# Eight chunks of a scan-and-adapters kernel: loads in 4 KB rows with woven 64-row transposes, and a re-searched order of its instructions

## The chip, the core and the metric

The kernel runs on 1 core of a Trainium2 chip. The metric is the device time in microseconds, the median of several runs. A profiled execution gives the times of single instructions.

## What is computed

The reference takes `a` and `b` of shape 8 x 6400 x 128 and runs a recurrence along the second axis. Its output `x`, seen as 51200 rows of 128, then goes through a mixture of eight adapters of rank 16, of which each row uses its two best:

```python
for t in range(S):
    h = a[:, t] * h + b[:, t]
    out[:, t] = h
...
logits = x @ w_gate
topk = np.argpartition(-logits, 2, axis=1)[:, :2]
w = softmax of the two selected logits
out = x + sum over the two of w[k] * ((x @ A[e]) @ B[e])
```

Input is 52.4 MB (`a` and `b`), output 26.2 MB.

## The kernel before

The 51200 rows are 100 chunks of 512. A chunk c goes through these steps, each an operation with a short name in the program (line numbers are those of the profile, which are the lines of the kernel before):

| name | engine | line | what |
|---|---|---|---|
| la, lb | SyncE queue | L710 | loads of a and b; from chunk 4 on, one load of 512 KB brings two chunks |
| A, B, P | TensorE | L731 | transposes of a into bank pA, of b into bank pB |
| ae | ScalarE | L749 | copy of pA into a_st |
| sc | VectorE | L787 | the scan over 512 steps: xT from a_st and pB; it needs the scan of the chunk before |
| Z | TensorE | L807 | xT times [A, w_gate] for a unit of 6 blocks of 128 rows, into pZ |
| ze | ScalarE | L813 | copy of pZ into zl |
| gate steps | VectorE, GpSimd, ScalarE | L844 to L883 | for a group of up to 4 units: the largest and the second largest logit, the weights g (sigmoid on ScalarE) |
| mu or md | GpSimd (L916) or VectorE (L920) | | product zw of zl and g |
| T | TensorE | L929 | transpose of zw into bank pO |
| te | VectorE (L938) or ScalarE (L935) | | copy of it into zwT |
| D | TensorE | L943, L944 | xT transposed back plus zwT times B, into pO |
| oe or od | ScalarE (L958) or VectorE (L955) | | copy of pO into outt |
| st | SyncE queue | L989 | store; one store of 512 KB takes two chunks, the last four chunks go one by one |

Of the gate steps, the two maxima and the last step (g, L883) are VectorE's; the others (kinds 2, 3, 5, 6 and 7: L844 to L875) are GpSimd's, but for those named in `GATE_DVE`. `TE_ACT`, `MU_DVE` and `OE_DVE` name the chunks whose zwT copy is ScalarE's, whose product is VectorE's, and whose outt copy is VectorE's.

Two layouts of a load occur (`load`, L695; `pieces`, L716). A flat chunk has 4 rows of 512 bytes to a partition, 2 KB in one piece, and its transposes are 4 of 128 x 128. In a woven pair, 8 rows, 4 KB in one piece, go to a partition; the first chunk of the pair lies on partitions 0 to 63, the second on 64 to 127. A woven chunk's transposes are 8 with 64 rows, and those of b of a chunk are woven with those of a of the next one, which lies on the other half of the partitions, to run side by side. Which layout a chunk has is decided by one line (L692):

```python
def woven(c):
    return HEAD <= c < NCH - TAIL and c // HC not in FLAT
```

`HEAD` is 4, `HC` is 2, `TAIL` is 0 and `FLAT` is [2, 3, 4, 5], so chunks 0 to 3 are flat in single loads of 256 KB, chunks 4 to 11 flat in pairs, and the others woven. There are buffers for 6 pairs (`NL`): a load waits until the transposes have read the pair that was there before. In `front` (L751), P is the woven group; A and B are the flat ones.

The order of the instructions on each engine is that of a rank (`schedule`, L333), sorted engine by engine:

```python
rank[op.i] = op.base + (TEMPLATE[op.kind][op.k] if op.kind in TEMPLATE else 0.0) + NUDGE.get(op.name, 0.0)
```

`TEMPLATE` holds an offset for each kind of operation and place in a period of 6 chunks, `NUDGE` one for each single operation; both come from a search. Each engine runs its list in that order, and an operation that must wait holds up what stands behind it. SyncE issues loads and stores from one list too. The store of chunks 68 and 69 is split (`SPLIT`) into parts of 124 and 4 rows of partitions.

Of the kernel before, what the change touches and what calls it, by code (L numbers as in the profile page):

```python
# [219 lines left out]
EARLY = -400  # L220
LEAD = [1, 2]
TAPER = [2, 1, 1, 1, 1]
GATE_DVE = ['2_14', '2_17', '2_18', '2_21', '3_14', '3_16', '5_17', '6_21', '7_16', '7_17', '7_18', '7_20', '7_21']
TAIL_UNITS = [4, 4, 4, 4]
HEAD_UNITS = [4, 4, 4]
FLAT = [2, 3, 4, 5]
# [56 lines left out]
    "q6": [0.0],  # L283
    "q7": [0.0],
    "q8": [0.0],
    "g7": [0.0],
    "g8": [0.0],
}

# [818 lines left out]
```

## Time and profile before

| | us |
|---|---|
| median of 3 runs | 203.43 (203.04 to 203.93) |
| profiled execution | 202.69 |
| its span | 200.7 |
| VectorE busy | 176.5 |
| ScalarE busy | 172.7 |
| GpSimd busy | 140.5 |

A profile has several views. The page gives busy totals, the span in 40 slices, the DMA queues, the chain of waits that ended last and the costliest groups of instructions. The windows view gives busy time, DMA share and rate for chosen stretches. The timeline lists instructions by start. The DMA view, cut to a stretch, lists what was issued in it, with the time from issue to landing.

### The profile page before, as it was taken

To read this page: it belongs to the slowest core of one execution; us is meant where nothing else is said; L and a number is where in the kernel's file an instruction comes from. 1 tells how busy PE (TensorE), PEld (TensorE's weight loads), DVE (VectorE), ACT (ScalarE), POOL (GpSimd) and SP (SyncE) were. 2 spreads that over 40 slices of the span, in tenths; PEclk is the share of its full clock that TensorE was granted. 3 is DMA by queue.
4 is the path that set the end of the run, shared out by engine and by line. 5 is a ranking of instruction groups with operands and counts; after the bars stand their busy time and mean duration, and the time that the engine had idled before them with its cause. 6 is when DMAs were issued, how large, how long until landed. Compare 5 with 4: busy or idle time off the path is not lost.

```text
span 200.7 us, 7490 instructions
## 1 busy us (share of the span) xinstructions
PE 180.8 (90%) x3128; PEld 157.9 (79%) x3128; DVE 176.5 (88%) x287; ACT 172.7 (86%) x317; POOL 140.5 (70%) x182
## 2 busy tenths in 40 slices
PE   6978999999999999899989999988879999998980
PEld 6868877888788888788878888877767887887860
DVE  1579999999999999999999999987888989999980
ACT  2548898999999998999899998986988998998971
POOL 1314559997888899797989798979678677744200
PEclk9999999999999999999999999999999999999997
DMA  5999999999999999999999999999999999999995
GB/s 213 382 391 389 412 406 411 398 416 407 406 410 414 405 411 412 416 411 407 408 414 408 409 418 407 407 411 414 410 413 411 410 414 410 404 384 379 352 371 225
DMA packets 30089, 79.26 MB, mean 395 GB/s; under 512 B 2664, under 2 KB 2920, under 8 KB 30056
## 3 DMA queue, kind: packets, MB, share of 16 engines
q1 hardware_dynamic: 29480, 78.39, 99.2%
q8 instruction: 25, 0.41, 0.8%
q10 hardware_dynamic: 576, 0.40, 0.6%
q14 instruction: 8, 0.07, 0.1%
HBM read 52.56 MB, written 26.21 MB: 393 GB/s over the span
## 4 chain that ended last, share of the span: by engine, by line
PE 21%; DVE 18%; DMA 13%; POOL 7%; ACT 3%; issue 2%; SPq 0%; DVEq 0%
DVE xT L787 9%; DMA b_tm<-in_b_dram 7%; DMA a_tm<-in_a_dram 6%; PE pZ L807 4%; POOL zw L916 4%; PE pA L731 4%; PE pB L731 3%; PE pO L929 3%; DVE zw L920 3%; PE pO L943 3%; PE pO L944 3%; DVE zwT L938 2%; ACT zl L813 1%; POOL L L846 1%; DVE g L883 1%
## 5 line engine op out<-in xcount | busy, mean ns | idle before, releaser
L787 DVE TENSOR_TENSOR_SCAN xT<-a_st,xT,pB 128x512 f16<-128x512 f32 x96 | 120.3, 1253 | 7.8 <-PE pB L731 3.7
L916 POOL TENSOR_TENSOR zw<-zl,g 128x512 f16<-128x512 f32 x87 | 92.0, 1068 | 21.9 <-DVE g L883 18.8
L731 PE MATMUL pB<-ident_f,b_tm 64*128 64x64 f32 (+1 forms) x752 | 68.3, 232 | 2.1 <-DMA a_tm<-in_a_dram 1.0
L731 PE MATMUL pA<-ident_f,a_tm 64*128 64x64 f32 (+1 forms) x752 | 68.2, 232 | 1.7 <-DMA b_tm<-in_b_dram 1.3
L749 ACT COPY a_st<-pA 128x512 f32<-128x512 f32 x100 | 59.9, 608 | 8.3 <-PE pA L731 5.9
L731 PEld LDWEIGHTS pA<-ident_f,a_tm 64*128 64x128 f32 (+1 forms) x752 | 55.7, 140 | 6.8 <-DMA b_tm<-in_b_dram 2.4
L813 ACT COPY zl<-pZ 128x816 f32<-128x816 f32 (+1 forms) x69 | 57.8, 838 | 3.7 <-PE pZ L807 3.5
L731 PEld LDWEIGHTS pB<-ident_f,b_tm 64*128 64x128 f32 (+1 forms) x752 | 55.2, 139 | 7.0 <-DMA a_tm<-in_a_dram 1.7
L958 ACT COPY outt<-pO 128x512 f32<-128x512 f32 x91 | 54.3, 609 | 3.3 <-PE pO L944 2.6
L943 PE MATMUL pO<-ident_h,xT 128*128 128x128 f16 x368 | 51.0, 221 | 0.5 <-ACT zwT L935 0.2
L944 PE MATMUL pO<-cst_h,zwT 128*128 128x128 f16 x368 | 50.3, 219 | 0.0
L943 PEld LDWEIGHTS pO<-ident_h,xT 128*128 128x128 f16 x368 | 40.7, 113 | 2.5 <-ACT zwT L935 0.4
L807 PE MATMUL pZ<-cst_h,xT 128*128 128x136 f16 x400 | 36.0, 225 | 6.4 <-ACT zl L813 2.7
L929 PE MATMUL pO<-ident_h,zw 128*128 128x128 f16 x368 | 35.5, 220 | 2.1 <-ACT outt L958 1.3
L944 PEld LDWEIGHTS pO<-cst_h,zwT 128*128 128x128 f16 x368 | 36.5, 99 | 0.0
L807 PEld LDWEIGHTS pZ<-cst_h,xT 128*128 128x128 f16 x400 | 26.3, 115 | 11.6 <-DVE xT L787 4.3
L938 DVE COPY zwT<-pO 128x512 f16<-128x512 f16 x72 | 29.2, 408 | 2.4 <-PE pO L929 2.0
L929 PEld LDWEIGHTS pO<-ident_h,zw 128*128 128x128 f16 x368 | 22.6, 97 | 6.2 <-issue 1.5
L846 POOL TENSOR_SCALAR L<-k 128x192 f32<-128x192 f32 (+2 forms) x15 | 12.2, 810 | 3.2 <-DVE k L844 2.0
L935 ACT COPY zwT<-pO 128x512 f16<-128x512 f16 x20 | 11.9, 603 | 1.3 <-PE pO L929 1.0
L787 DVE TENSOR_TENSOR_SCAN xT<-a_st,pB 128x512 f16<-128x512 f32 (+1 forms) x8 | 7.5, 937 | 4.9 <-ACT a_st L749 4.7
L853 POOL TENSOR_TENSOR L<-k,m 128x192 f32<-128x192 f32 (+2 forms) x17 | 8.5, 500 | 2.5 <-DVE m L851 2.4
(56 smaller groups left out, 110.8 us busy)
## 6 DMA issues: line engine op xcount, KB each, us to landing
a_tm<-in_a_dram SPq DMA_DIRECT2D x48, 512.0 KB, 13.2
b_tm<-in_b_dram SPq DMA_DIRECT2D x48, 512.0 KB, 13.3
out_dram<-outt SPq DMA_DIRECT2D x47, 512.0 KB, 13.4
a_tm<-in_a_dram SPq DMA_DIRECT2D x4, 256.0 KB, 4.2
out_dram<-outt SPq DMA_DIRECT2D x4, 256.0 KB, 3.6
b_tm<-in_b_dram SPq DMA_DIRECT2D x3, 256.0 KB, 4.8
out_dram<-outt SPq DMA_DIRECT2D x1, 496.0 KB
b_tm<-in_b_dram ACTq DMA_DIRECT2D x1, 256.0 KB, 3.5
```

The costliest lines, as they stand in the source:

```text
L731: last = eng["pe"].transpose(*args)
L749: lambda: eng["act"].copy(a_st[c % NA][:, :], pA[:, c % 2, :]), fr(c, "ae"))
L787: last = eng["dve"].tensor_tensor_scan(out=x[:, s0:s1], data0=a_st[c % NA][:, s0:s1], data1=pB[:, c % 2, s0:s1], initial=init, op0=ALU.mul ...
L807: last = eng["pe"].matmul(pZ[:, k // (n // 2), o : o + W], xblock(b0 + k), Awg_h)
L813: return eng["act"].copy(zl[:, zb : zb + n, :].rearrange("p (h k) w -> p h (k w)", h=2), pZ[:, :, 0 : n // 2 * W])
L846: lambda e: e.tensor_scalar(out=ll, in0=kk, scalar1=0.0, scalar2=-1.0e30, op0=ALU.is_ge, op1=ALU.mult))
L916: lambda: eng["pool"].tensor_tensor(out=wv, in0=zv, in1=gv, op=ALU.mult), ba(gi, c, "mu"))
L929: last = eng["pe"].transpose(ptile[:, k * 128 : k * 128 + 128], zz[:, k, :], ident_h[:, :])
L938: lambda: eng["dve"].tensor_copy(zt, ptile[:, 0 : n * 128]), ba(gi, c, "te"))
L943: eng["pe"].matmul(dst, xblock(b0 + k), ident_h[:, :], start=True, stop=False)
L944: last = eng["pe"].matmul(dst, zt[:, k * 128 : k * 128 + 128], B_h, start=False, stop=True)
L958: lambda: eng["act"].copy(ov, bv), ba(gi, c, "oe"))
```

## The change

`FLAT` becomes empty: chunks 4 to 11 are loaded in 4 KB rows and transposed in woven groups. `TE_ACT` names 33 chunks for 25, `MU_DVE` 14 for 13, `OE_DVE` 6 for 2, `GATE_DVE` 21 steps for 13. `TEMPLATE` and `NUDGE` get other values. No function changes.

```diff
 NUDGE = {
-    "A0": 404.647, "A1": 403.572, "A10": 13.623, "A11": 14.602, "A12": 9.931, "A2": 403.247, "A3": 402.602, "A4":
+    "A0": 223.948, "A1": 270.971, "A2": 361.165, "A3": 453.348, "A4": 152.944, "B0": 349.945, "B1": 298.534, "B2":
...
-GATE_DVE = ['2_14', '2_17', '2_18', '2_21', '3_14', '3_16', '5_17', '6_21', '7_16', '7_17', '7_18', '7_20', '7_21']
+GATE_DVE = ['2_14', '2_17', '2_18', '2_21', '3_11', '3_13', '3_15', '3_16', '3_8', '5_1', '5_14', '5_17', '6_1', '6_18', '7_0', '7_1', '7_17', '7_18', '7_20', '7_21', '7_3']
...
-FLAT = [2, 3, 4, 5]
+FLAT = []
 FILL = {}
-TE_ACT = [1, 7, 13, 19, 25, 31, 37, 43, 49, 55, 61, 67, 73, 78, 80, 82, 83, 84, 89, 91, 92, 94, 96, 97, 98]
-MU_DVE = [82, 84, 86, 90, 91, 92, 93, 94, 95, 96, 97, 98, 99]
-OE_DVE = [95, 97]
+TE_ACT = [0, 1, 2, 7, 12, 15, 19, 22, 25, 31, 37, 43, 49, 55, 59, 61, 67, 68, 69, 73, 75, 78, 80, 82, 83, 87, 91, 92, 94, 95, 96, 97, 98]
+MU_DVE = [1, 61, 72, 77, 82, 84, 86, 91, 92, 93, 94, 96, 97, 99]
+OE_DVE = [15, 72, 93, 95, 96, 97]
...
 TEMPLATE = {
-    "la": [0.0, 0.0, 0.0],
-    "lb": [0.0, 0.0, 0.0],
+    "la": [7.292, -18.475, 1.959],
+    "lb": [-2.36, 20.502, -2.697],
...
-    "ae": [0.0, 0.0, 0.0, 0.0, 0.0, 0.0],
+    "ae": [-0.158, -1.349, -2.394, -1.722, -1.554, -1.285],
```

The lists that come of it, by name (a digit after "g" or "q" is the gate step, the number behind the underscore the group; "g" is on VectorE, "q" on GpSimd). SyncE's list at its beginning and near its end:

```text
before  la0 la1 lb1 la2 lb2 la3 lb3 la4 lb4 la6 lb6 la8 lb8 lb10 la10 la12 lb12 la14 lb14 la16
after   la0 la1 lb1 la2 la4 lb2 la3 lb3 lb4 la6 lb6 lb8 la8 la10 la12 lb10 lb12 la14 lb16 lb14
...
before  la88 la84 st50 lb84 lb86 la86 st52 st54 lb88 la92 la90 lb90 st56 lb94 lb92 la94 st58 st60 la96 lb96 la98 st62 lb98 st64
after   la84 lb84 la86 st50 lb86 la88 lb88 st52 st54 la90 lb90 st56 la92 lb92 st58 la94 lb94 la96 st60 lb96 st62 la98 lb98 st64
```

VectorE's list behind the last scan:

```text
before  sc99 te87 g7_17 md91 g2_18 g8_17 g7_18 te86 md90 md95 g1_19 te90 te88 md92 g8_19 md94 md93 g8_18 g1_21 g1_20 te93 te95 g2_21 g7_20 md97 g8_20 g6_21 g7_21 md98 od95 g8_21 md99 md96 te99 od97
after   sc99 g6_18 g2_18 g7_17 g7_18 md91 g8_17 te86 g1_19 te89 te90 te88 md92 g8_19 md94 g8_18 md93 g1_20 g1_21 te93 g2_21 g7_20 md97 g8_20 od95 od93 g7_21 md96 g8_21 md99 te99 od97 od96
```

GpSimd's list at the end:

```text
before  mu85 q6_16 q3_17 mu87 mu89 q6_18 q6_17 mu88 q2_19 q6_19 q7_19 q6_20 q2_20
after   mu85 q6_16 q7_16 q3_17 mu87 mu89 mu88 q6_17 mu90 q2_19 q6_19 mu95 q7_19 q6_20 q2_20 q6_21 mu98
```

From about chunk 16 to chunk 90 the lists of TensorE differ little.

More of the change, by code (lines that the diff above doesn't have):

```diff
@@ L246 @@
 TEMPLATE = {
-    "la": [0.0, 0.0, 0.0],
-    "lb": [0.0, 0.0, 0.0],
-    "A": [0.0, 0.0, 0.0, 0.0, 0.0, 0.0],
-    "B": [0.0, 0.0, 0.0, 0.0, 0.0, 0.0],
-    "ae": [0.0, 0.0, 0.0, 0.0, 0.0, 0.0],
-    "sc": [0.0, 0.0, 0.0, 0.0, 0.0, 0.0],
-    "Z": [0.0, 0.0, 0.0, 0.0],
-    "ze": [0.0, 0.0, 0.0, 0.0],
-    "g1": [0.0],
-    "g2": [0.0],
-    "g3": [0.0],
-    "g4": [0.0],
-    "g5": [0.0],
-    "g6": [0.0],
-    "w1": [0.0],
+    "la": [7.292, -18.475, 1.959],
+    "lb": [-2.36, 20.502, -2.697],
+    "A": [0.0, 0.0, 0.0, 0.0, -77.131, 0.0],
+    "B": [6.476, 115.991, 1.619, 2.053, 0.8, 0.266],
+    "ae": [-0.158, -1.349, -2.394, -1.722, -1.554, -1.285],
+    "sc": [103.035, 162.331, 73.569, 125.536, 113.13, -41.329],
+    "Z": [-0.392, 1.405, 1.616, 1.351],
+    "ze": [-0.475, -1.793, -1.762, -1.437],
+    "g1": [4.417],
+    "g2": [17.713],
+    "g3": [-31.479],
+    "g4": [55.654],
+    "g5": [47.657],
+    "g6": [-84.906],
+    "w1": [-2.483],
     "w2": [0.0],
@@ L265 @@
     "p3": [0.0],
-    "mu": [0.0, 0.0, 0.0, 0.0, 0.0, 0.0],
-    "T": [0.0, 0.0, 0.0, 0.0, 0.0, 0.0],
-    "te": [0.0, 0.0, 0.0, 0.0, 0.0, 0.0],
-    "D": [0.0, 0.0, 0.0, 0.0, 0.0, 0.0],
-    "oe": [0.0, 0.0, 0.0, 0.0, 0.0, 0.0],
-    "st": [0.0, 0.0, 0.0],
-    "ta": [0.0, 0.0, 0.0, 0.0, 0.0, 0.0],
-    "md": [0.0, 0.0, 0.0, 0.0, 0.0, 0.0],
+    "mu": [64.351, 160.215, 442.91, 203.787, 287.661, 429.055],
+    "T": [1.552, 1.177, 1.789, 0.902, -0.174, 0.02],
+    "te": [51.303, 131.399, -52.317, 105.995, -5.732, -28.829],
+    "D": [0.885, 1.521, 1.324, -0.392, 0.257, 1.318],
+    "oe": [-2.698, -1.786, -1.96, -0.083, -1.166, -1.669],
+    "st": [12.662, 11.623, 10.72],
+    "ta": [60.514, -0.994, 74.852, -2.187, 0.213, 32.426],
+    "md": [-27.973, 2.278, 1.381, 326.409, 54.424, 29.225],
     "wu": [0.0],
     "fi": [0.0, 0.0, 0.0, 0.0, 0.0, 0.0],
-    "ch": [0.0],
-    "cm": [0.0],
-    "cc": [0.0],
+    "ch": [40.503],
+    "cm": [120.223],
+    "cc": [-6.567],
     "mb": [0.0],
-    "q2": [0.0],
-    "q3": [0.0],
-    "q5": [0.0],
-    "q6": [0.0],
-    "q7": [0.0],
+    "q2": [78.255],
+    "q3": [65.225],
+    "q5": [-46.707],
+    "q6": [92.869],
+    "q7": [115.224],
     "q8": [0.0],
-    "g7": [0.0],
-    "g8": [0.0],
+    "g7": [58.4],
+    "g8": [-63.561],
 }
```

361 rows, old and new, of the table NUDGE are left out of this document.

## The prediction

> **What bounds the kernel now.** I read the page first: the engine totals, the slices, the DMA queues.
>
> ```profile
> PE 180.8 (90%) x3128; PEld 157.9 (79%) x3128; DVE 176.5 (88%) x287; ACT 172.7 (86%) x317; POOL 140.5 (70%) x182
> ...
> DMA  5999999999999999999999999999999999999995
> GB/s 213 382 391 389 412 406 411 398 416 407 406 410 414 405 411 412 416 411 407 408 414 408 409 418 407 407 411 414 410 413 411 410 414 410 404 384 379 352 371 225
> ...
> q1 hardware_dynamic: 29480, 78.39, 99.2%
> ```
>
> No engine is as full as the DMA queue of SyncE: its packets fill 99.2% of the 16 engines' span. The rate line has three levels: about 390 GB/s in the slices to 20 us, about 411 in the middle, 350 to 385 at the end. The windows view puts numbers on them (columns: stretch, its length, busy us of PE, PEld, DVE, ACT, POOL, clock, DMA share, GB/s).
>
> ```profile
> 8.00:18.00 10.00, 7.74 (x75) 6.83 (x74) 8.29 (x14) 5.69 (x12) 1.77 (x4) 1.00 1.05 389
> 20.00:29.00 9.00, 8.70 (x138) 7.63 (x135) 8.75 (x12) 8.41 (x16) 5.68 (x9) 1.00 1.02 406
> 60.00:160.00 100.00, 92.67 (x1759) 81.60 (x1756) 92.06 (x134) 91.04 (x166) 85.00 (x101) 1.00 1.03 411
> 170.00:180.00 10.00, 9.60 (x175) 8.27 (x172) 9.97 (x19) 9.98 (x20) 6.17 (x8) 1.00 1.03 397
> 185.00:190.00 5.00, 4.59 (x76) 4.07 (x73) 4.83 (x23) 5.00 (x12) 0.96 (x5) 1.00 0.93 354
> ```
>
> From 8 to 18 us the chip moves loads in 2 KB rows at 389 GB/s with the share already at 1.05; from 20 to 29 us loads in 4 KB rows at 406; from 60 to 160 us two loads in 4 KB rows to one store in 2 KB rows at 411. DVE and ACT, loose in the middle (92 and 91%), are full from 170 to 190 us. So the end has two candidates: the DMA and the two engines. The DMA view, cut to single issues, decides between them (KB, us from issue to landing).
>
> ```profile
> 163.13 1.87 SPq L710 DMA_DIRECT2D b_tm<-in_b_dram  x1
> ...
> b_tm<-in_b_dram SPq DMA_DIRECT2D x1, 512.0 KB, 13.8
> ```
>
> ```profile
> out_dram<-outt SPq DMA_DIRECT2D x1, 512.0 KB, 4.8
> ```
>
> ```profile
> out_dram<-outt SPq DMA_DIRECT2D x1, 256.0 KB, 2.9
> ```
>
> The last load (b of chunks 98 and 99) is issued at 163.13 and lands 13.8 later, at 176.9. The second row is the store of chunks 94 and 95, issued between 192.80 and 192.85, landed at 197.6. The third is the last store, issued between 197.27 and 197.30, landed at 200.2. Behind the last load lie the stores of 36 chunks, 9.44 MB: 23.3 us, or 405 GB/s. At 411 it would be 23.0. So although the share falls to 0.93, the queue delivers to its end at nearly its steady pace; what is idle then are some of the 16 engines while others still drain. A sentence of the Trainium skill fits that: by "DMA: Bandwidth & Descriptors", section "Why a DMA increments its semaphore by 16 and not by 1", a DMA uses the largest number of engines up to 16 that divides its outer sizes, so the 124-row part of the store of chunks 68 and 69 would run on 4; the falling share at an unbroken pace agrees with that.
>
> Compute ends at almost the same moment. The last scan starts at 181.31, 4.4 us behind the last landing, and the last outt copy at 196.02:
>
> ```profile
> 181.31 1.27 DVE L787 TENSOR_TENSOR_SCAN xT<-a_st,xT,pB 128x512 f16<-128x512 f32 x1
> ```
>
> ```profile
> 196.02 0.59 ACT L958 COPY outt<-pA 128x512 f32<-128x512 f32 x1
> ```
>
> So the kernel is bound by DMA throughout, and the tail's compute keeps within a few tenths of it. The profiled execution took 202.69 (span 200.7, 2.0 around it), 0.74 under the median of 203.43; I work out differences and subtract them from the median.
>
> **The change, part by part.** *Row size.* Chunks 4 to 11 are eight loads of 512 KB. Before, their pace can be read from two of them:
>
> ```profile
> 4.00 0.45 SPq L710 DMA_DIRECT2D a_tm<-in_a_dram  x1
> ...
> 8.17 2.46 SPq L710 DMA_DIRECT2D a_tm<-in_a_dram  x2
> ```
>
> ```profile
> a_tm<-in_a_dram SPq DMA_DIRECT2D x1, 512.0 KB, 6.1
> ```
>
> ```profile
> a_tm<-in_a_dram SPq DMA_DIRECT2D x1, 512.0 KB, 11.4
> ```
>
> The a load of chunks 4 and 5 lands at 4.00 + 6.1 = 10.1, that of 10 and 11 (the first of the two at 8.17) at 19.6, seven loads later: 1.36 each. By rates, 0.524 MB at 389 GB/s is 1.35, at 406 it is 1.29, at 411 1.28. Eight loads save 8 x 0.06 = 0.45 to 8 x 0.08 = 0.65; I take 0.55, and since the queue never runs dry behind them it all reaches the last load. The Trainium skill speaks for less: the same page, "Why small descriptors are slow (HBM only)", gives 3 cycles for each packet beside one per 32 bytes, so 67 for 2 KB and 131 for 4 KB, a gain of 2.3% or an estimated 0.24 us in all; the rows above show 5%, and they decide.
>
> *Woven transposes.* Two flat groups of 4 (A and B of one chunk) take 0.44 us each from start to start, a woven group of 16, which does as much, about 0.71:
>
> ```profile
> 18.22 0.61 PE L731 MATMUL pA<-ident_f,a_tm 128*128 128x128 f32 x4
> 18.66 0.60 PE L731 MATMUL pB<-ident_f,b_tm 128*128 128x128 f32 x4
> 19.10 0.52 PE L807 MATMUL pZ<-cst_h,xT 128*128 128x136 f16 x6
> ```
>
> ```profile
> 151.99 0.27 PE L731 MATMUL pA<-ident_f,a_tm 64*128 64x64 f32 x1
> ...
> 152.63 0.40 PE L929 MATMUL pO<-ident_h,zw 128*128 128x128 f16 x4
> ```
>
> That is 0.88 against 0.64 of pitch (151.99 to 152.63), so eight chunks free up to 2 us of PE, which is only 77% busy from 8 to 18 us while it waits for data. A woven group needs a of the next chunk beside b of its own, so a chunk can wait one load (1.3) longer. Neither reaches the end, because the loads run on: nothing in the head is late for the DMA, whose queue holds 11 us at 8.17 and 13.8 at 163. If that cover went, a head 2 us late would cost 2 us less what is gained back in the middle; I cost it at 0.
>
> *Order of the head.* The a load of chunks 4 and 5 goes ahead of b of chunk 2, so chunks 2 and 3 come one 512 KB load (1.3 us) later; DVE is busy only 8.29 of 10 us there. The bytes ahead of the first store are the same 30 issues. Cost 0, by the same cover.
>
> *More on ScalarE, and the gates.* Counted from the two programs' orders, ScalarE copies zwT 33 times for 25 and outt 94 for 98; VectorE loses 8 zwT copies and gains 4 outt copies, 1 product zw and 8 gate steps; GpSimd loses 1 product and 8 gate steps.
>
> ```profile
> L916 POOL TENSOR_TENSOR zw<-zl,g 128x512 f16<-128x512 f32 x87 | 92.0, 1068 | 21.9 <-DVE g L883 18.8
> ...
> L958 ACT COPY outt<-pO 128x512 f32<-128x512 f32 x91 | 54.3, 609 | 3.3 <-PE pO L944 2.6
> ...
> L938 DVE COPY zwT<-pO 128x512 f16<-128x512 f16 x72 | 29.2, 408 | 2.4 <-PE pO L929 2.0
> ...
> L935 ACT COPY zwT<-pO 128x512 f16<-128x512 f16 x20 | 11.9, 603 | 1.3 <-PE pO L929 1.0
> ```
>
> ```profile
> L920 DVE TENSOR_TENSOR zw<-zl,g 128x512 f16<-128x512 f32 x13 | 8.6, 682 | 0.0
> ...
> L955 DVE COPY outt<-pO 128x512 f32<-128x512 f32 x1 | 0.7, 683 | 0.0
> ```
>
> ACT: 8 x 0.603 - 4 x 0.609 = +2.4 us. DVE: -8 x 0.408 + 5 x 0.68 = +0.1, plus 8 gate steps between the small and the wide ones. Over 200 us both have the room (172.7 and 176.5 busy), and it lies in the head and the middle: 0.
>
> *The tail.* Behind the last scan VectorE loses three zw products (chunks 90, 95 and 98, now GpSimd's) and two zwT copies and a gate step, and gains two outt copies (93 and 96), a zwT copy and a gate step: -3 x 0.68 - 0.41 + 2 x 0.68 = -1.1 us. ScalarE there goes from 24 copies to 22, -1.2. The load of b for chunks 92 and 93 stands 125 issues down instead of 126, the last one at 134 in both. So tail compute comes at least 0.55 (data) and up to 1.1 more ahead. Of that the DMA lets through only what it delivers under pace, 23.3 against 23.0: 0 to 0.3. I take 0.15, the middle.
>
> **Sum:** -0.55 - 0.15 = -0.7: 202.0 for the profiled execution, **202.7** for the median.
>
> **The rivals.** *Compute sets the end.* For it: DVE and ACT are full from 170 to 190, the share falls to 0.93, and the chain of waits ends on the outt copy quoted above, not on a transfer. Against it: the landings keep 405 GB/s. If it holds, the end moves by data and tail work together, 0.55 + 1.1 = 1.65, less up to 0.4 where GpSimd's slower product enters: -1.2 to -1.7, about **202.0**.
>
> *GpSimd becomes the tail's bound (slower).* Chunks 90, 95 and 98 cost 1.07 there, not 0.68, and when VectorE holds its operands more: one took 1.61 at 178.66. The sum that feeds group 19's sigmoid (chunk 97) now stands behind chunk 95's product on GpSimd; VectorE's step that makes the group's weights waits for that sigmoid, and behind it on VectorE stand five products and four outt copies, with the last stores behind those.
>
> ```profile
> 178.66 1.61 POOL L916 TENSOR_TENSOR zw<-zl,g 128x512 f16<-128x512 f32 x1 [0.90 <-DVE g L883]
> ...
> 186.27 0.24 POOL L869 TENSOR_TENSOR k<-zl,v 128x32 f32<-128x32 f32 x1 [3.13 <-DVE v L858]
> ```
>
> If all three come on the chain, 3 x 1.61 = 4.8 less the 1.1 taken off VectorE and the 0.55: +3.1, near 206.5; if two do, +1.6, **205.0**. It decides once GpSimd is late by more than the 1.65 that the tail gains. Against it: GpSimd idles 3.13 ahead of 186.27.
>
> *The rows bring nothing.* 389 GB/s could be the rate of the start, whatever the rows: then -0.15 or nothing, **203.3**. For it: the first 8 us run no faster (382). Against it: the jump to 406 comes where the rows change, with stores still absent.
>
> **How the numbers follow.** Forecast 0.50 (own range 202.2 to 203.1, with the bounds of both terms and the spread of the runs, of which 0.08 lies past -1.0); compute sets the end 0.25; GpSimd 0.12; rows bring nothing 0.13. Half a percent, 1.0 us, is about what a measurement of this kernel can tell from no change. Faster: 0.25 + 0.08 = 0.33. Slower: 0.10 of the GpSimd case, the rest of it being milder, and 0.02 of the fourth: 0.12. Within: 0.42 + 0.02 + 0.11 = 0.55. The range takes in -1.9 and part of the slower side: 201.5 to 204.5.
>
> **What would show it.** Right: from 8 to 18 us over 400 GB/s; the last load landing near 176.3, not 176.9; its distance to the last landing still 23.0 to 23.3; the last outt copy over a microsecond earlier with a longer way from issue to landing for the last stores. The distance shrinking to 22.3 or less shows that compute set the end. Stalls of VectorE behind 183 us on GpSimd show the slower rival. An unchanged rate from 8 to 18 us would make the forecast wrong at its first term; a DMA share under 0.95 anywhere from 20 to 160 us, because a late head starves the queue, would make the cover wrong.

## The result, and the profile after

| | before | after |
|---|---|---|
| median | 203.31 us (202.80 to 203.93, 20 runs) | 202.88 us (202.28 to 203.47, 20 runs) |
| ratio | | 0.9976, 95% interval 0.9966 to 0.9987 |
| profiled execution, its span | 202.69, 200.7 us | 203.03, 201.0 us |

The changed kernel is 0.49 us faster by the ratio (0.26 to 0.69 by its interval). The two profiled executions stand the other way round, 0.3 apart: single executions of one kernel differ by more than that, so single times of the two traces are compared below only where they differ by more or where another kernel shows the same.

The page of the changed kernel (busy totals, rate by slice, DMA queues) reads almost as before. Line numbers are 3 lower in it.

```profile
PE 179.8 (89%) x3192; PEld 156.3 (78%) x3192; DVE 177.3 (88%) x292; ACT 173.4 (86%) x321; POOL 135.5 (67%) x173
...
GB/s 214 371 415 408 408 408 408 402 412 409 412 402 415 404 410 413 409 414 405 410 410 411 407 414 412 407 410 406 414 409 410 415 410 416 394 385 383 326 328 252
...
q1 hardware_dynamic: 28456, 78.39, 98.7%
```

The third slice is at 415 instead of 391, and there are 1,024 packets fewer for the same 78.39 MB. The windows view, in the stretches that the prediction read, shows both what was gained and what the tail looks like (stretch, its length, busy us of PE, PEld, DVE, ACT, POOL, clock, DMA share, GB/s):

```profile
8.00:18.00 10.00, 7.49 (x106) 5.87 (x104) 9.47 (x16) 6.47 (x13) 2.21 (x5) 1.00 1.03 412
20.00:29.00 9.00, 7.54 (x144) 6.38 (x144) 8.52 (x12) 8.05 (x15) 3.87 (x6) 1.00 1.03 409
60.00:160.00 100.00, 95.61 (x1813) 84.46 (x1814) 93.78 (x140) 94.36 (x175) 81.33 (x97) 1.00 1.03 410
170.00:180.00 10.00, 9.08 (x164) 7.72 (x165) 9.86 (x18) 9.43 (x19) 6.45 (x9) 1.00 1.02 394
185.00:190.00 5.00, 4.51 (x81) 4.31 (x79) 4.06 (x18) 5.00 (x13) 2.68 (x5) 1.00 0.85 328
```

From 8 to 18 us the rate went from 389 to 412 GB/s. From 20 to 160 us hardly anything changed. From 185 to 190 us the rate fell from 354 to 328 and VectorE idles 0.9 us of 5, where it idled 0.2. The timeline and the DMA view, cut to single issues, give the end:

```profile
162.98 1.22 SPq L707 DMA_DIRECT2D b_tm<-in_b_dram  x1
...
182.51 1.27 DVE L784 TENSOR_TENSOR_SCAN xT<-a_st,xT,pB 128x512 f16<-128x512 f32 x1
...
196.65 0.69 DVE L952 COPY outt<-pA 128x512 f32<-128x512 f32 x1 [0.58 <-PE pA L941]
...
197.51 0.65 SPq L986 DMA_DIRECT2D out_dram<-outt  x1
```

```profile
b_tm<-in_b_dram SPq DMA_DIRECT2D x1, 512.0 KB, 13.6
```

```profile
out_dram<-outt SPq DMA_DIRECT2D x1, 256.0 KB, 3.1
```

The last load lands at 162.98 + 13.6 = 176.6, before 176.9. The last scan, though, starts at 182.51 instead of 181.31, and the last outt copy ends at 197.34 instead of 196.61. So compute came 0.7 to 1.2 us later in this execution, not earlier as predicted, and the last store lands at 197.51 + 3.1 = 200.6. It is not this execution alone: in the five traces of kernels with the new order (below) it is 22.1 to 23.0 us from scan 88 to scan 99, in the nine with the old one 21.0 to 21.2. The experiments had to say why a kernel whose compute is later is still faster.

### The profile page after: what moved, and what is told of

The parts are those of the page before. It is cut to its first block, busy times and chain, and to the rows that moved or that the text cites. A ratio compares the mean times of both kernels' runs of the same rounds, so it can differ in the third digit from the quotient of the medians.

```text
span 201.0 us, 7618 instructions
## 1 busy us (share of the span) xinstructions
PE 179.8 (89%) x3192; PEld 156.3 (78%) x3192; DVE 177.3 (88%) x292; ACT 173.4 (86%) x321; POOL 135.5 (67%) x173
## 3 DMA queue, kind: packets, MB, share of 16 engines
q1 hardware_dynamic: 28456, 78.39, 98.7%
## 4 chain that ended last, share of the span: by engine, by line
PE 39%; ACT 22%; DMA 17%; DVE 8%; POOL 6%; issue 5%; ACTq 1%; POOLq 1%; SPq 0%; DVEq 0%
DMA a_tm<-in_a_dram 14%; ACT zl L810 8%; PE pB L728 7%; PE pA L728 7%; PE pZ L804 7%; ACT outt L955 6%; ACT a_st L746 6%; PE pO L940 6%; PE pO L926 6%; PE pO L941 4%; DVE xT L784 4%; POOL zw L913 3%; DMA cst_f<-in_moe_B_dram 3%; ACT zwT L932 2%; DVE zwT L935 2%
## 5 line engine op out<-in xcount | busy, mean ns | idle before, releaser
L728 PE MATMUL pB<-ident_f,b_tm 64*128 64x64 f32 (+1 forms) x784 | 69.3, 230 | 2.7 <-DMA a_tm<-in_a_dram 1.4
L728 PE MATMUL pA<-ident_f,a_tm 64*128 64x64 f32 (+1 forms) x784 | 70.1, 231 | 1.8 <-issue 1.6
L746 ACT COPY a_st<-pA 128x512 f32<-128x512 f32 x100 | 61.0, 614 | 7.6 <-PE pA L728 5.4
L728 PEld LDWEIGHTS pB<-ident_f,b_tm 64*128 64x128 f32 (+1 forms) x784 | 56.6, 139 | 8.4 <-issue 2.6
L728 PEld LDWEIGHTS pA<-ident_f,a_tm 64*128 64x128 f32 (+1 forms) x784 | 56.9, 139 | 6.8 <-issue 1.7
L935 DVE COPY zwT<-pO 128x512 f16<-128x512 f16 x64 | 25.8, 410 | 3.4 <-PE pO L926 3.4
L932 ACT COPY zwT<-pO 128x512 f16<-128x512 f16 x28 | 16.7, 610 | 3.4 <-PE pO L926 3.3
L843 POOL TENSOR_SCALAR L<-k 128x192 f32<-128x192 f32 (+2 forms) x12 | 9.6, 799 | 3.4 <-DVE k L841 2.5
L846 POOL TENSOR_TENSOR L<-L,k 128x192 f32<-128x192 f32 x14 | 8.7, 621 | 3.7 <-DVE L L843 2.9
L841 POOL TENSOR_TENSOR k<-zl,m 128x192 f32<-128x192 f32 (+1 forms) x15 | 7.6, 505 | 3.9 <-DVE m L859 3.9
```

What stands on the lines that cost most here:

```text
L728: last = eng["pe"].transpose(*args)
L746: lambda: eng["act"].copy(a_st[c % NA][:, :], pA[:, c % 2, :]), fr(c, "ae"))
L932: lambda: eng["act"].copy(zt, ptile[:, 0 : n * 128]), ba(gi, c, "ta"))
L935: lambda: eng["dve"].tensor_copy(zt, ptile[:, 0 : n * 128]), ba(gi, c, "te"))
```

## The experiments

The theory under test: the landings of the last stores set the end, so the row size counts in full and compute's place behind the last scan counts nothing as long as it isn't too late. The rivals: compute sets the end; GpSimd or the new order does. The twelve kernels below carry the order of each engine as a list written out, taken from the kernel that they are made from, so that one thing can be changed and the rest stays. All were timed in five rounds; before was 203.26 to 203.32 beside them.

| label | what | median us (lowest to highest) | ratio to before, 95% interval |
|---|---|---|---|
| rows_only | before, 4 KB rows alone | 202.77 (202.40 to 203.22) | 0.9971 (0.9951 to 0.9991) |
| order_only | after, rows flat again | 203.72 (203.44 to 204.25) | 1.0019 (1.0005 to 1.0034) |
| rows_tail | rows_only with after's tail | 202.79 (202.25 to 203.66) | 0.9971 (0.9956 to 0.9987) |
| before_light | before, less work in the tail | 203.36 (202.72 to 204.09) | 0.9999 (0.9980 to 1.0019) |
| after_light | after, less work in the tail | 203.00 (202.55 to 203.70) | 0.9982 (0.9967 to 0.9997) |
| rows_light | rows_only, less work in the tail | 202.93 (202.77 to 203.79) | 0.9986 (0.9973 to 0.9999) |
| before_heavy | before, two more products in the tail | 203.74 (203.20 to 204.13) | 1.0016 (1.0002 to 1.0031) |
| rows_nosplit | rows_only, store 68 not split | 203.37 (203.17 to 204.07) | 1.0012 (0.9996 to 1.0028) |
| rows_relief | rows_only, store 66 split too | 203.31 (202.80 to 204.01) | 1.0000 (0.9982 to 1.0018) |
| rows_relief_light | the same, less work in the tail | 203.32 (202.80 to 203.99) | 0.9997 (0.9983 to 1.0011) |
| after_loads | after, load la4 at its old place | 203.02 (202.53 to 204.52) | 0.9994 (0.9972 to 1.0016) |
| after_head | after, la4 at its old place, the constant's cast later | 203.11 (202.68 to 204.10) | 0.9992 (0.9975 to 1.0008) |

**Rows against order.** In rows_only TensorE's list has the woven groups P4 to P11, each at the place of the later of the two flat groups that it replaces; order_only is the changed kernel with the flat groups put back the same way.

```diff
-FLAT = [2, 3, 4, 5]
+FLAT = []
```

> The kernel before with only the row size changed: chunks 4 to 11 in 4 KB rows and woven groups, each woven group at the place of the later of the two flat groups that it replaces, every other instruction where it was. Theory 1 (the DMA queue sets the time, and eight loads save 0.45 to 0.65 us): the last load lands 0.45 to 0.65 us earlier than before (near 176.3), the time falls by 0.4 to 0.7 us. Theory 2 (the rows bring nothing by themselves, the new order does): the last load lands within 0.2 us of before and the time is within 0.2 us of before. Theory 3 (the woven groups, which wait for a load more, make the head late and cost it back): the last load lands earlier but the time is the same or up to 0.5 us longer.

> The changed kernel with the old rows: chunks 4 to 11 flat in 2 KB rows, every woven group replaced by its two flat groups in place, the new order and engine choice kept. Theory 1: 0.45 to 0.65 us slower than the changed kernel, so at or up to 0.2 us above the time of before. Theory 2: as fast as the changed kernel, 0.4 us under before. Theory 3: faster than the changed kernel.

The windows view from 8 to 18 us, first of rows_only, then of order_only:

```profile
8.00:18.00 10.00, 7.03 (x99) 5.54 (x99) 7.72 (x12) 5.48 (x12) 1.66 (x4) 1.00 1.03 413
```

```profile
8.00:18.00 10.00, 9.18 (x88) 7.52 (x86) 9.55 (x16) 6.96 (x14) 2.19 (x5) 1.00 1.05 393
```

The rate goes with the rows, 412 and 413 against 389 and 393, whichever order stands around them. In time, the rows bring 0.5 us in the order of before (203.29 to 202.77) and 0.8 in the order of after (203.72 to 202.88). The 0.8 is more than the 0.45 to 0.65 expected, though the two intervals leave room for that. The new order by itself costs 0.4 with flat rows (its interval lies above 1); with 4 KB rows it is 202.77 against 202.88, which these runs don't tell from nothing.

**The tail by itself.** rows_tail is rows_only with the changed kernel's choices and lists from scan 92 on:

```diff
-GATE_DVE = [..., '5_17', '6_21', '7_16', '7_17', '7_18', '7_20', '7_21']
+GATE_DVE = [..., '5_17', '6_18', '7_17', '7_18', '7_20', '7_21']
...
-TE_ACT = [..., 83, 84, 89, 91, 92, 94, 96, 97, 98]
-MU_DVE = [82, 84, 86, 90, 91, 92, 93, 94, 95, 96, 97, 98, 99]
-OE_DVE = [95, 97]
+TE_ACT = [..., 83, 87, 91, 92, 94, 95, 96, 97, 98]
+MU_DVE = [82, 84, 86, 91, 92, 93, 94, 96, 97, 99]
+OE_DVE = [93, 95, 96, 97]
```

> The rows-only kernel with the changed kernel's choices and order from the last scans on (which copies and products are on ScalarE, VectorE and GpSimd): the tail step of the prediction by itself. The prediction gave it 0 to -0.3 us: 202.5 to 202.8 against 202.77. If the DMA engines set the end, nothing (202.6 to 202.9), even where the last copies end 0.5 to 1.6 us earlier. If the shift to GpSimd and the other order is what costs the changed kernel its 0.1, or makes GpSimd the tail's bound, later: 202.9 to 203.5, with VectorE waiting for GpSimd behind 183 us.

The timeline of rows_only, and the DMA view of its last issue:

```profile
181.02 1.27 DVE L862 TENSOR_TENSOR_SCAN xT<-a_st,xT,pB 128x512 f16<-128x512 f32 x1
...
195.73 0.58 ACT L1033 COPY outt<-pA 128x512 f32<-128x512 f32 x1
...
197.03 0.86 SPq L1064 DMA_DIRECT2D out_dram<-outt  x1
```

```profile
out_dram<-outt SPq DMA_DIRECT2D x1, 256.0 KB, 3.2
```

The same of rows_tail:

```profile
180.78 1.26 DVE L862 TENSOR_TENSOR_SCAN xT<-a_st,xT,pB 128x512 f16<-128x512 f32 x1
...
194.91 0.69 DVE L1030 COPY outt<-pA 128x512 f32<-128x512 f32 x1 [0.58 <-PE pA L1019]
...
196.38 1.12 SPq L1064 DMA_DIRECT2D out_dram<-outt  x1
```

```profile
out_dram<-outt SPq DMA_DIRECT2D x1, 256.0 KB, 4.3
```

Here compute does come earlier: the last copy ends at 195.60 instead of 196.31, the last store is issued 0.65 earlier, and it takes 4.3 instead of 3.2 us. It lands at 200.7, the other at 200.2. All of the gain is given back between issue and landing, and the medians are 202.79 and 202.77. The tail step is worth nothing that these runs can tell.

**Taking work out of the tail.** The light kernels leave out the adapters' share of chunks 90 to 99 (no product, T or zwT copy there; D only transposes xT back):

```diff
+            if ch >= 90:
...
+                        last = eng["pe"].matmul(bank[:, k * 128 : k * 128 + 128], xblock(b0 + k), ident_h[:, :], start=True, stop=True)
...
+                return copy_out(gi, ch, c, b0, n, bank)
```

> The kernel before, leaving out the adapters' share of chunks 90 to 99: no product, transpose or copy of zw for them, their output is x alone. All loads and stores stay. VectorE loses ten products and about four copies behind the last scan, some 7 us. If the DMA queue sets the end (theory 1), the time falls by 0 to 0.4 us, and the distance from the last load's landing to the last landing stays at 23.0 to 23.3 us. If compute sets the end, the time falls by more than 0.8 us.

> The changed kernel, leaving out the adapters' share of chunks 90 to 99 in the same way. Theory 1: 0 to 0.4 us under the changed kernel, and 0.3 to 0.6 us under the same cut of the kernel before, since the rows' gain then shows whole. If compute sets the end in the changed kernel, it falls by more than 0.8 us, to the same time as the cut of the kernel before less 0.3.

> The rows-only kernel with the adapters' share of chunks 90 to 99 left out, so that the compute behind the last scan ends about 3 to 4 us earlier and the output is not the reference's in those chunks. If the landings of the last stores set the end (my theory), 202.5 to 203.0 us, within 0.2 of the rows-only kernel's 202.77. If the rows-only kernel's end is set by compute, so that the time that the rows save can only be had up to there, at least 0.5 less: 202.3 or lower. The same cut was worth nothing in the kernel before (203.36 against 203.3) and nothing in the changed kernel (203.00 against 202.88).

The windows view of rows_light, the last copy on its timeline, and the DMA view of its last issue (it stands at 196.12 in the trace):

```profile
185.00:190.00 5.00, 4.05 (x62) 3.41 (x60) 1.99 (x17) 4.83 (x12) 0.90 (x4) 1.00 0.96 369
190.00:195.00 5.00, 0.60 (x8) 0.44 (x8) 1.34 (x3) 1.97 (x5) 0.00 (x0) 0.72 1.02 388
```

```profile
191.30 0.67 ACT L1044 COPY outt<-pA 128x512 f32<-128x512 f32 x1
```

```profile
out_dram<-outt SPq DMA_DIRECT2D x1, 256.0 KB, 4.6
```

The last copy ends at 192.0, 4.3 us before that of rows_only, and the last store still lands at 196.1 + 4.6 = 200.7. All three cuts move the median by less than 0.2, upward if at all. So what compute does in the tail doesn't set the end of any of the three kernels.

**What does.** A DMA leaves 16 landing records in the trace. The time of the last of the 16, for the ten stores that land last, in order:

```text
before      191.20 192.49 193.70 194.99 196.32 197.63 198.34 198.97 199.60 200.22
after       191.36 192.65 193.93 195.25 196.54 197.90 198.56 199.26 199.92 200.56
rows_only   191.07 192.34 193.66 195.10 196.38 197.67 198.31 198.97 199.60 200.24
rows_tail   191.46 192.76 194.01 195.40 196.76 198.05 198.70 199.35 200.00 200.64
rows_light  191.38 192.66 194.03 195.44 196.79 198.07 198.76 199.39 200.03 200.67
order_only  192.05 193.45 194.80 196.16 197.54 198.81 199.91 200.55 201.17 201.78
after_head  191.07 192.35 193.64 195.88 197.13 198.37 199.00 199.62 200.27 200.90
```

In the first five rows the steps are 1.3 us for 512 KB and 0.64 for the last four of 256 KB, without a gap: whatever lands last never waits for compute. The other landings do: the median of the 16 for the last store is 199.5 in before, 199.8 in after, 199.1 in rows_tail and 198.8 in rows_light. It follows the issue by 2.2 to 2.7 us, and is 0.7 to 1.9 us ahead of the last one. The end is that of the latest of 16, and by this reading a store may be late by about that lead before it counts. In order_only a step of 1.10 stands where 0.64 is usual, in after_head one of 2.24 where 1.3 is: there the latest landing had to wait for a store, 0.5 and 0.9 us. These two have the latest last scans, 183.13 and 183.37. Not all of order_only's lateness is the tail's: its profiled execution is the slowest of its twelve (204.25), with 331 GB/s from 3 to 8 us and the last load landing only at 178.1.

**Adding work to the tail** checks that lead from the other side: before_heavy computes the products of chunks 91 and 92 twice on VectorE, once into a spare tile.

```diff
-lambda: eng["dve"].tensor_tensor(out=wv, in0=zv, in1=gv, op=ALU.mult)
+lambda: [eng["dve"].tensor_tensor(out=o, in0=zv, in1=gv, op=ALU.mult) for o in ([spare...] if c in (91, 92) else []) + [wv]][-1]
```

> The kernel before with two zw products more on VectorE in the tail (those of chunks 91 and 92 done twice, the extra ones into a tile that nothing reads): 2 x 0.68 = 1.4 us, of which 1.2 in pitch. If compute is within a few tenths of the DMA there, as the prediction says: 0.6 to 1.2 us slower than before. If the DMA has the whole end to itself with a microsecond to spare: within 0.3 us of before.

```profile
197.16 0.59 ACT L1034 COPY outt<-pA 128x512 f32<-128x512 f32 x1
```

Two products of 0.68 put the last copy at 197.16 instead of 196.02, 1.1 later, and cost 0.5 us in the median, 0.3 by the ratio (0.04 to 0.63), between the two expectations. If all lateness beyond the lead counts, an estimate is that some 0.7 us of it were free in before (0.5 to 1.1). The profiled execution itself shows no gap in its last landings, so this rests on the medians alone, and the way in which the work costs time is not shown.

**Which of the 16 is late.** rows_nosplit stores chunks 68 and 69 in one part; the relief kernels split the store of 66 and 67 too.

```diff
-SPLIT = {68: [124, 4]}
+SPLIT = {}
```

```diff
-SPLIT = {68: [124, 4]}
+SPLIT = {66: [120, 8], 68: [124, 4]}
```

> The kernel before with 4 KB rows alone (as in rows_only), and the store of chunks 68 and 69 in one piece on all engines of the DMA. Theory 1 in its sharper form (one of the 16 DMA engines, the one that lands last, sets the end; the split store spares it 16 packets of 2 KB, some 1.3 us): 0.6 to 1.2 us slower than rows_only, 203.4 to 204.0, with the spread of the 16 landings of the last stores 1 us or more. If the pace of the whole queue sets the end and the engines are alike: within 0.2 us of rows_only.

> The same with 4 KB rows alone, the store of 68 and 69 split as before, and the store of chunks 66 and 67 split into 120 and 8 rows of partitions, which by a rule of the Trainium skill leaves the last of the 16 DMA engines out of its larger part (page DMA: Bandwidth & Descriptors, section Why a DMA increments its semaphore by 16 and not by 1). If that one is the slowest, theory 1 gives 0.2 to 0.6 us less than rows_only (202.2 to 202.6), and then the next engines or compute set the end. If the slowest is another one: within 0.2 us, 202.7 to 203.0. If the pace of the whole queue sets the end: 0 to 0.1 us slower.

> The same cut, and the last load but one is split so that its 120 rows go to 8 DMA engines and 8 rows to the others, as the last one's 124 rows already go to 4. Without the cut this second split gave 203.31, 0.5 above the rows-only kernel, with compute later in its profile. If the engine that ends last is one that the second split spares, 0.5 us or more below the cut kernel without it: 202.0 to 202.4. If the late engine is another one from run to run, or the total of bytes sets the end, the same as the cut kernel without it within 0.3, or later by up to 0.5, since 8 engines then carry 15 rows each where they carried 8.

Taking the split away costs 0.6 us, as much as the rows bring, and the two intervals don't overlap. Compute is the same (its last copy stands at 195.74), the last store is issued earlier and takes longer:

```profile
196.35 0.33 SPq L1064 DMA_DIRECT2D out_dram<-outt  x1
```

```profile
out_dram<-outt SPq DMA_DIRECT2D x1, 256.0 KB, 4.8
```

Its 16 landings: 14 within 0.16 us of the first, one 1.64 behind, one 2.85. One late landing out of 16 is the end of that kernel. The second split brought nothing, with or without the cut: 203.31 is 0.5 over rows_only, slower than each of its three expectations, and 203.32 is 0.4 over rows_light; both intervals overlap those of the kernels without it. (The expectation for the cut one calls it a load that goes to 8 engines; it is the store of chunks 66 and 67. In both relief traces its two parts together leave 23 landings, besides one record at the end of each issue, where two whole DMAs leave 32: that fits 15 engines for the 120 rows and 8 for the 8 rows. The parts of 124 and 4 rows leave eight, four each: 178.63 to 179.29 and 180.16 to 181.17 us in before.) So the split at 68 is worth 0.6 us and a further one nothing; which engine is late after the first stays open.

**The head.** after_loads puts la4 behind lb3 again, after_head moves the cast of a constant on VectorE too, from ahead of the first scan to behind the second (not the third, as its expectation says; in before it stands behind the fourth):

```diff
-la2 la4 lb2 la3 lb3 lb4
+la2 lb2 la3 lb3 la4 lb4
...
-own ch sc0 sc1 sc2
+own sc0 sc1 ch sc2
```

> The changed kernel with one load moved: a of chunks 4 and 5 behind b of chunk 3, where it stood before, instead of ahead of b of chunk 2. If the new order costs what it costs (0.1 to 0.4 us) in the first 8 us of the queue, where the constants load beside it: the rate from 3 to 8 us goes from 361 up to 380 GB/s and the time falls by 0.1 to 0.4 us, to rows_only (202.6 to 202.8). If the order costs elsewhere: within 0.1 us of the changed kernel.

> The changed kernel with two moves at the head undone: load la4 behind lb3 on SyncE's queue, and the cast of the constant behind the third scan on VectorE, where it stood first and held scan 0 for 1.35 us. If the head's order costs what the changed kernel lacks against the rows-only kernel, 202.7 to 202.8, with the first scans some 1.3 us earlier; if the backlog of scans is made later, or the DMA engines hide it, the changed kernel's 202.9 within 0.2.

VectorE's timeline in the changed kernel, and then in after_head:

```profile
8.14 0.23 DVE L615 CAST cst_h<-cst_f 128x136 f16<-128x136 f32 x1 [5.93 <-DMA cst_f<-in_moe_B_dram]
8.28 1.21 DVE L784 TENSOR_TENSOR_SCAN xT<-a_st,pB 128x512 f16<-128x512 f32 x1
```

```profile
7.27 1.22 DVE L858 TENSOR_TENSOR_SCAN xT<-a_st,pB 128x512 f16<-128x512 f32 x1 [5.06 <-PE pB L802]
```

In the changed kernel the first scan stands behind the cast, which waits for its constant. In after_head it comes 1.0 us earlier. Most of that isn't the cast's: in after_loads, with the cast still ahead, the first scan starts at 7.42. The rate from 3 to 8 us didn't rise with la4 moved (354 GB/s in after_loads, 361 in after), and the time is no better in either: 203.02 and 203.11 against 202.88. So the order of the head isn't seen to cost anything.

## Why the prediction was right, point by point

**Bound by DMA: right, and more strictly than written.** The prediction read the tail's 405 GB/s as a pace 0.3 us short of the 411 of the middle, which compute could fill. It isn't the pace of the queue. The DMA view of before from 176 to 200.3 us counts less than the 9.44 MB:

```profile
DMA packets 4382, 8.43 MB, mean 347 GB/s; under 512 B 292, under 2 KB 292, under 8 KB 4378
```

The rest had moved before the last load's latest landing, on engines that were up to 5.9 us ahead. The unbroken pace is that of the latest landings, 1.3 us for 512 KB. The cut kernels show that less compute fills nothing. The sentence that some engines idle while others drain was the right one, and its consequence, that compute in the tail has no price as long as it isn't late by more than the estimated 0.7 us, wasn't drawn. The rule of the Trainium skill that the prediction names there ("DMA: Bandwidth & Descriptors", "Why a DMA increments its semaphore by 16 and not by 1") agrees with the four landings of each part of the split store; no run here shows which engines a part goes to. The falling share, which the prediction took for a sign of that split, is none: from 185 to 190 us it is 0.86 in rows_nosplit, without the split, and 0.90 in rows_only.

**Row size, -0.55: right.** Eight loads of 0.524 MB at 391 instead of 412 GB/s are 0.55 us; rows_only measured 0.59 by its ratio (0.18 to 1.00). The rival that the rows bring nothing falls with the 413 GB/s in rows_only and 393 in order_only. Of the two estimates of the gain by row the trace's 5% was nearer than the 2.3% that follows from the Trainium skill, "DMA: Bandwidth & Descriptors", section "Why small descriptors are slow (HBM only)": measured are 5 to 6%.

**Woven transposes and the order of the head, 0: right**, by rows_only, where the rows' gain comes whole with the woven groups, by the 1.03 of DMA share from 20 to 160 us, and by the two head kernels. (The prediction gives a woven group 0.71 and then 0.64 us; TensorE gains 1.4 or 1.9 us over eight chunks, and either way it costs nothing.)

**More on ScalarE, "it lies in the head and the middle: 0": the working failed, the zero nearly held.** Two of the operations that VectorE gained, by name of chunks 72 and 77, don't run with those chunks. They stand between scans 88 and 89. VectorE in the changed kernel:

```profile
159.48 1.27 DVE L784 TENSOR_TENSOR_SCAN xT<-a_st,xT,pB 128x512 f16<-128x512 f32 x1
160.85 0.69 DVE L952 COPY outt<-pO 128x512 f32<-128x512 f32 x1
161.46 0.68 DVE L917 TENSOR_TENSOR zw<-zl,g 128x512 f16<-128x512 f32 x1
162.06 1.27 DVE L784 TENSOR_TENSOR_SCAN xT<-a_st,xT,pB 128x512 f16<-128x512 f32 x1
```

and in rows_only:

```profile
159.85 1.28 DVE L862 TENSOR_TENSOR_SCAN xT<-a_st,xT,pB 128x512 f16<-128x512 f32 x1 [0.29 <-PE pB L806]
161.05 0.33 DVE L937 TENSOR_REDUCE m<-zl 128x24 f32<-128x192 f32 x1
161.63 1.28 DVE L862 TENSOR_TENSOR_SCAN xT<-a_st,xT,pB 128x512 f16<-128x512 f32 x1 [0.26 <-PE pA L806]
```

From scan 88 to 89 it is 2.58 us against 1.78: 0.8 lost, and it isn't made up: from scan 88 to scan 99 it is 23.03 against 21.17. That is more than the 0.55 of "data" in the prediction's tail. The new order as a whole costs 0.4 with flat rows (order_only), and not measurably with 4 KB rows; that these two operations are what costs it is not shown, since no run moves them alone.

**The tail, -0.15: wrong in both of its steps, and small.** Compute comes earlier by 1.1 plus 0.55, the prediction said. Behind the last scan the lists do save, but from the last scan's start to the end of the last copy it is 14.83 us in after and 15.30 in before: 0.47, since VectorE now waits for TensorE where it didn't, here and, for 0.58, ahead of the last copy:

```profile
186.52 0.42 DVE L935 COPY zwT<-pO 128x512 f16<-128x512 f16 x1 [0.79 <-PE pO L926]
...
195.04 0.42 DVE L935 COPY zwT<-pB 128x512 f16<-128x512 f16 x1 [0.49 <-PE pB L926]
```

With the later scans that ends 0.7 late. And where compute does come earlier, by 0.7 in rows_tail and by 4.3 in rows_light, it brings nothing.

**The rivals.** Compute sets the end (202.0): no, by the three cut kernels. GpSimd becomes the tail's bound: no. VectorE's waits behind 181 us are all for TensorE, and GpSimd idles 2.5 us ahead of a step there:

```profile
190.22 0.25 POOL L868 TENSOR_TENSOR L<-zl,v 128x32 f32<-128x32 f32 x1 [2.54 <-DVE v L855]
```

Of the marks that the prediction named, the rate came out as written. The last load landed 0.3 us earlier, not 0.6, which single executions can't tell: in before_light and before_heavy, with the loads of before, it lands at 177.8 and 176.6. The last copy over a microsecond earlier didn't come, nor did the distance of 23.0 to 23.3: it is 200.6 - 176.6 = 24.0, in before 23.3, and 23.6 to 24.7 in the other kernels; before_light, rows_light and after_light, with little compute, have 23.6, 24.1 and 24.4. So the distance is no measure of compute.

**The sum** of -0.7 stands against -0.49 (-0.69 to -0.26): the rows as predicted, the tail nothing. Whether the order takes back another 0.1 can't be told from these runs. The wide range, 201.5 to 204.5, would have held with no change at all; what was tested is the rows' term. No kernel tried was clearly faster than the changed one; rows_only, at 202.77, is the simplest that is as fast.

## What to carry to other kernels

Where a queue of large transfers is full to the end, ask which of its engines ends last and whether that one ever waits, before pricing any work of the tail: cut the tail's compute once and see whether the time moves. A longer way from issue to landing with an earlier issue is the mark of it in a profile. And what an operation costs is read from where it stands in its engine's list, not from the chunk in its name.

## What the runs showed of the hardware

The 16 landings of one load lie 0.3 us apart at 10 to 19 us in before, 1.7 apart at 25 us, and 5.9 at the last load; in the other kernels 5.5 to 6.5 at the last load. The landings drift apart over the run. One candidate for the cause is the queue that the page of before calls instruction,

```profile
q8 instruction: 25, 0.41, 0.8%
```

whose 25 packets of 16 KB take 0.8% of 16 engines' span, 0.8% x 16 x 201 / 25 = 1.0 us each, and can't fall evenly on 16. The traces bear part of it out. The first of these packets runs at 19.27 us in before, 18.82 in after and 16.69 in rows_only; about there the latest landing of a load comes 2.4 to 2.7 us behind that of the load before instead of 1.3, and the spread of the 16 grows by 1.1 to 1.4. It grows by 1.2 to 1.4 again about the ninth packet (77.77, 77.36 and 76.63). Eleven of the fourteen traces show the first such step, and eleven the second. The growth from 3.3 to 5.9 isn't accounted for, and no run moved these packets, so that they are the cause is not shown.

The first microseconds differ from execution to execution with the same head: from 3 to 8 us before moved 381 GB/s and before_light, identical there, 313. The last landing of the profiled executions varies by a microsecond with it, which is more than the whole change brings; only the medians of many runs could carry this study.
